# Joining turned sums on GpSimd instead of ScalarE, with more buffers and earlier row loads, in an attention-and-GEGLU block

## The chip, the core and the metric

The kernel runs on one core of a Trainium2 chip. Its engines are TensorE (PE for matmuls and PEld for weight loads in the profile), VectorE (DVE), ScalarE (ACT), GpSimd (POOL) and SyncE (SP), whose queue issues nearly all DMAs. The metric is the time of one execution in device microseconds (us), as the median of several runs.

## What is computed

```python
h = layernorm(x) * (1 + ca) + sa
x = x + ga * attention(h)           # 32 query heads, 8 key/value heads, 512 cached keys, 2048 queries
h = layernorm(x) * (1 + cb) + sb
x = x + gb * ((gelu(h @ w_gate) * (h @ w_up)) @ w_down)
```

`x` is 2048 x 512, the inner width of the second part is 1792, and `sa, ca, ga, sb, cb, gb` are rows of 512 that follow from a condition vector. Everything is float32. The kernel splits each operand into two float16 parts (high and low) and makes three matmuls for one product (`mm3`, L86 to L90).

## The kernel before

The attention part takes some 1330 us of the span and is not touched. The change lies in the second part, the gated network, which the kernel works through in two passes, one for each half of the 2048 rows. A pass is generation g = 0 or 1; it holds 1024 rows, as two blocks `qb` of 512 rows, each of four tiles of 128 rows (QT = 4, QB = 512).

The inner width of 1792 is cut into seven pairs of 128-column tiles (NP = 7). Pair n of a pass has two sets, q = 2n (gate) and 2n + 1 (up). `f_items` (L1264) makes the seven products of a set, in the way of Strassen, in PSUM tiles `fa`, `fb`, `fc`. ScalarE copies them out (L885), VectorE adds and multiplies (L1270, L1287), ScalarE applies the gelu (L1276) and makes the high part of the result `at` (L1297), and the low part is made by L1298, on VectorE or GpSimd.

The product with `w_down` then goes one of two ways:

- The first five pairs of a pass are "turned" (L293). `yt_tasks` (L1696) makes seven products for each of two column halves p, in the order `YORDER`, with the result transposed: the 512 output columns lie along the partitions. `yt_add` (L1653) adds each, scaled by a column, into eight running sums `YT[g, c, qb]` of 128 x 512 (c is the column tile, 0 to 3). They live in the eight buffers of the tag `acc`.
- The last two pairs (NROW = 2) use `y_tasks` (L940): the result lies in rows, in PSUM tiles `py`, and VectorE adds it straight into the tile of rows `acc[ti]` (L952).

After the fifth pair the turned sums must come back to rows. `post` (L1710) sees that a sum got its last addend (`LAST`) and puts off `yt_turn` (L1662). Its `split` (L1666) has ScalarE part the 32-bit sums into low and high 16-bit halves, the "parting" `yu`; its `turn` (L1671) has SP issue a DMA transpose of it into `yv`. There are three buffers for `yu` (tag `qt`). When four sums are parted, the residual rows `y1[ti]` of one block are loaded by `load_acc` (L98) into `acc[ti]`, three ticks later, in buffers of the tag `acc` that parted sums have left. `yt_row` (L1681) then, for each of four row tiles of a block, joins the halves again: ScalarE copies `yv` into `yr` (L1686), a 128 x 1024 copy of 16-bit numbers that takes its two halves from places 1024 bytes apart, and GpSimd adds `yr` to the residual rows (L1687). `yr` lies in the tag `raw`, of five buffers. A tile of rows is written out (L1647 and L1649) when it has this and its two `py` addends (`f_final`, L1641).

What sets the order: the SP queue issues strictly in the order in which the Python code emits. The loop at L1727 emits seven steps for each set and calls `tick` after each; `put_off(n, f)` runs f after n ticks. On the other engines a scheduler places the instructions of this part by its own estimate of times, so the built program's order on them may differ from the order of emission; each engine then works through its own list in order. PSUM has five buffers for the tag `acc` (NACC), which `py`, `fb`, `fc` and the turned products share.

Of the kernel before, what the change touches and what calls it, by code (L numbers as in the profile page):

```python
# [10 lines left out]
F32 = mybir.dt.float32  # L11
F16 = mybir.dt.float16
U16 = mybir.dt.uint16
BF16 = mybir.dt.bfloat16
AF = mybir.ActivationFunctionType
# [3 lines left out]
P = 128  # L19
S, D, F = 2048, 512, 1792  # L20
HQ, HKV, DH = 32, 8, 128
W = 512
KT = D // P
NF = F // P
NT = S // P
QB = 512
QT = QB // P
# [18 lines left out]
NRW = 2  # L46
NWR = 2
# [17 lines left out]
def block_kernel(ctx: ExitStack, tc: tile.TileContext, x, kT, v, wq, wo, wg, wu, wd, cT, wc, wm, out):  # L65
    nc = tc.nc

    const = ctx.enter_context(tc.tile_pool(name="const", bufs=1))
    pool = ctx.enter_context(tc.tile_pool(name="pool", bufs=2))
# [7 lines left out]
    def raw(name):  # L77
        return pool.tile([P, 512], F32, tag="raw", name=name, bufs=NRAW)
# [7 lines left out]
    def mm3(ps, lhi, llo, rhi, rlo, first, last, chain=False, left=False):  # L86

        order = ((lhi, rlo), (lhi, rhi), (llo, rhi)) if left else ((llo, rhi), (lhi, rhi), (lhi, rlo))
        for n, (a, b) in enumerate(order):
            nc.tensor.matmul(ps, a, b, start=first and n == 0, stop=last and n == 2, skip_group_check=chain)  # L90

    acc, moved, bg = {}, [0], []
# [2 lines left out]
        moved[0] += 1  # L95
        nc.sync.dma_start(out_, in_)

    def load_acc(i, src, eng=None):  # L98
        acc[i] = pool.tile([P, D], F32, tag="acc", name="acc", bufs=2 * QT)
        (eng.dma_start if eng else dma)(acc[i], src)  # L100

    def rows_of(t, i):
# [4 lines left out]
    for i in range(QT):  # L107
        load_acc(i, rows_of(x, i), nc.scalar if i < 2 else None)
# [246 lines left out]
    BK, hs, y1 = {}, {}, {}  # L355
# [100 lines left out]
    def put_off(n, fn):  # L456

        waits_.append([n, fn])
# [415 lines left out]
    def banks(st, tags):  # L874
        def bk(k):
            def get():
                if k not in st:
                    st[k] = bank(*tags[k])
                return st[k]
            return get  # L880
        return bk
# [76 lines left out]
    def attn_final(ti):  # L958
        y1[ti] = dram.tile([P, D], F32, name=f"y{ti}")
        dma(y1[ti], acc[ti])  # L960
        if ti < 2 * QT:
            nxt = ti + 2 * QT
            own, steps = ln_tile(2, ti, lambda: acc[ti])
            own()
            for d, fn in zip((1, 5, 8, 9, 10, 12, 13), steps):
                at(("w", now[0] + d), fn)
            at(now[0] + 12, lambda: load_acc(nxt, rows_of(x, nxt)))
        else:
            ln_last(ti - 2 * QT)
# [63 lines left out]
    for i in range(QT, 2 * QT):  # L1033
        load_acc(i, rows_of(x, i))
# [175 lines left out]
    for g in range(NG):  # L1210
# [9 lines left out]
        elif g >= GW and (not half or pr < GW):  # L1220
            sched_set(g, srcs, t0, by, spread)
            if not half:
                a, b, c, d, e, f = SETPOS2 if g == GW else SETPOS
# [312 lines left out]
    with tc.manual_schedule():  # L1536
        begin()
        nexty, invs = [], {}
        for t in range(T + TAIL):
            now[0] = t  # L1540
            u, s = divmod(t, 4)
# [83 lines left out]
    for i in range(2 * QT):  # L1625
        q = 7 * (2 + i // 2) + 3 * (i % 2)
# [7 lines left out]
    for p in range(2):  # L1634
        q = 51 + 14 * p
# [5 lines left out]
    def f_final(ti):  # L1641
        assert ti in back
        halfway[ti] = halfway.get(ti, 0) + 1
        if halfway[ti] <= NROW:
            return
        if ti >= 2 * QT:
            dma(rows_of(out, ti), acc[ti])  # L1647
        else:
            put_off(2, lambda: dma(rows_of(out, ti), acc[ti]))  # L1649

    YT, YR, back, halfway = {}, {}, set(), {}

    def yt_add(n, c, qb, ps):  # L1653
        by = ST["dyc"][:, KT * (n % NP) + c:KT * (n % NP) + c + 1]
        key = (n // NP, c, qb)
        if key in YT:
            nc.vector.scalar_tensor_tensor(YT[key], ps, by, YT[key], op0=ALU.mult, op1=ALU.add)  # L1657
        else:
            YT[key] = pool.tile([P, QB], F32, tag="acc", name="yt", bufs=2 * QT)
            nc.vector.tensor_scalar(YT[key], ps, by, None, op0=ALU.mult)  # L1660

    def yt_turn(g, c, qb):  # L1662

        def split():
            u = YR["u", c, qb] = pool.tile([P, 2, QB], U16, tag="qt", name="yu", bufs=3)
            nc.scalar.activation(u, YT[g, c, qb].bitcast(U16).rearrange("p (r h) -> p h r", h=2), AF.Copy)  # L1666

        def turn():
            if ("t", qb) not in YR:
                YR["t", qb] = pool.tile([P, KT, 2 * QT, P], U16, tag="pt", name="yv", bufs=NPT)  # L1670
            nc.sync.dma_start_transpose(YR["t", qb][:, c], YR.pop(("u", c, qb)).rearrange("p a b -> p (a b)"))  # L1671

        split()
        put_off(3, turn)
        YR["n"] = YR.get("n", 0) + 1
        if YR["n"] % QT == 0:
            for i in range(QT):
                ti = 2 * QT * g + (YR["n"] - 1) % (2 * QT) // QT * QT + i
                put_off(3, lambda ti=ti: load_acc(ti, y1[ti]) or back.add(ti))

    def yt_row(g, qb, i):  # L1681
        t = YR["t", qb].rearrange("p c (h i) q -> p c q h i", h=2)
        ti = 2 * QT * g + QT * qb + i
        assert ti in back
        r = raw("yr")
        nc.scalar.activation(r.bitcast(U16).rearrange("p (c q h) -> p c q h", c=KT, h=2), t[:, :, :, :, i], AF.Copy)  # L1686
        nc.gpsimd.tensor_tensor(acc[ti], acc[ti], r, op=ALU.add)  # L1687
        f_final(ti)
        if i == QT - 1:
            del YR["t", qb]  # L1690

    ADDS = {1: ((0, 0),), 2: ((0, 0),), 6: ((0, 1),), 5: ((1, 1),), 7: ((1, 1),), 4: ((1, 0),), 3: ((0, 1),)}
    YORDER = (1, 2, 6, 5, 7, 3, 4)
    LAST = {2: (0, 0), 7: (1, 1), 3: (0, 1), 4: (1, 0)}

    def yt_tasks(n):  # L1696
        tasks = []
        for p in range(2):
            st = {}
            bk = banks(st, {"a": ("acc", "ya", NACC) if p else ("qa", "ya", 1), "b": ("acc", "yb", NACC), "c": ("acc", "yc", NACC)})  # L1700

            def group(k, p=p, bk=bk):
                a, b = PROD[k]
                x, start = CHAIN[k]
                ci, off = YCOL[a]
                w, t = WO["f", n, ci], A[n, {"b11": "11", "b21": "21", "b22": "22"}.get(b, b)]
                sl = slice(off + p * P, off + (p + 1) * P)
                mm3(bk(x)(), w[:, 0, sl], w[:, 1, sl], t[:, 0, :], t[:, 1, :], start, k in (2, 4, 3), True)

            def post(k, p=p, st=st):  # L1710
                (i, qb), = ADDS[k]
                yt_add(n, 2 * i + p, qb, st[CHAIN[k][0]])
                if n % NP == NP - NROW - 1 and k in LAST:
                    i, qb = LAST[k]
                    c, g = 2 * i + p, n // NP
                    put_off(2 if k in (3, 4) and p == k // 4 else 1, lambda: yt_turn(g, c, qb))
                    if p and k in (3, 4):
                        for r in range(QT):
                            put_off((9 if k == 4 else 13) + r, lambda r=r: yt_row(g, qb, r))

            tasks += [(lambda k=k, f=group: f(k), lambda k=k, f=post: f(k)) for k in YORDER]
        return [tasks[k:k + 2] for k in range(0, len(tasks), 2)]

    YCOL = {"a11": (0, 0), "a12": (0, 256), "s2": (1, 0), "s3": (1, 256), "s4": (2, 0), "s1": (2, 256), "a22": (3, 0)}
# [2 lines left out]
    for q in range(NQ):  # L1727
        n, m = divmod(q, 2)
        its = items(NG + q) if q < 2 else f_items(q)
        for k, pk in enumerate(ORDER):  # L1730
            if (q, pk) not in f_done:
                all_of(its[pk])
            run(("f", q, k))
            tick()
            if n and k == 2 and m == 0 and turned(n - 1):
                nexty += yt_tasks(n - 1)
            if k in ((1, 2, 5, 6) if q < NQ - 1 else (1, 5)):
                y_next()
        if m == 1 and not turned(n):
            for qi, (a, b) in enumerate((("11", "21"), ("12", "22"))):  # L1740
                for i in range(QT):
                    nexty.append(y_tasks((2 * (n // NP) + qi) * QT + i, [lambda n=n, a=a: A[n, a], lambda n=n, b=b: A[n, b]],
                                         [("f", n, 0), ("f", n, 1)], col("dysc", n % NP), f_final))
# [40 lines left out]
```

## Time and profile before

| | |
|---|---|
| median of 3 runs | 1745.58 us (1743.76 to 1745.96) |
| profiled execution | 1743.57 us |
| its span, first to last instruction | 1741.8 us |
| granted TensorE clock | 1.00 throughout |
| second part, pass 0 turned back | about 1485 to 1531 us of the span |
| second part, pass 1 turned back | about 1677 to 1726 us of the span |

Times in the views count from the start of the span. In a row of a timeline the columns are start, duration, engine, line, operation, output and inputs, how many are merged, and in brackets the idle time of the engine before it and what ended that. The table by stretches gives for each stretch its length and the busy time and instruction count of PE, PEld, DVE, ACT and POOL, then the granted clock, the busy share of the DMA engines and GB/s.

### The profile page before, as it was taken

The page shows a single profiled execution, that of the slowest core. Times are in us where ns is not written, and L with a number is a line of the kernel's source. Part 1 is how long each engine was busy: PE and PEld are TensorE (multiplying, and loading weights), DVE is VectorE, ACT ScalarE, POOL GpSimd, SP SyncE. Part 2 cuts the span into 40 slices and gives each one's busy share as a digit, 9 for nine tenths or more (in the row PEclk, how much of TensorE's full clock was granted, in tenths as well). Part 3 has the DMA queues.
Part 4 walks back from the last instruction along what each step waited for, and adds up shares of the span by engine and source line. Part 5 has one row for each costly group of instructions (what it writes and reads, how often), then busy time and mean ns, then how long its engine had stood idle before and what let it go on. Part 6 is the DMA issues. An engine that isn't in the chain of part 4 may idle for free.

```text
span 1741.8 us, 26188 instructions
## 1 busy us (share of the span) xinstructions
PE 1714.7 (98%) x8022; PEld 787.0 (45%) x8022; DVE 1417.6 (81%) x2454; ACT 1258.5 (72%) x2813; POOL 1045.9 (60%) x1266
## 2 busy tenths in 40 slices
PE   7999999999999999999999999999999999999998
PEld 5444444444444444444444444444444444444443
DVE  7898898888888899888888788888886678556674
ACT  6988788888878777898778778787784554643344
POOL 4889778776788884654675665754621558313422
PEclk9999999999999999999999999999999999999999
DMA  7999999999999999999999999899986663743235
GB/s 236 218 205 211 213 214 207 223 206 221 215 217 228 205 205 187 212 213 230 201 219 224 208 223 220 186 235 218 197 180 150 187 177 128 191 139 100 91 97 167
DMA packets 690636, 339.82 MB, mean 195 GB/s; under 512 B 578880, under 2 KB 601408, under 8 KB 690496
## 3 DMA queue, kind: packets, MB, share of 16 engines
q1 hardware_dynamic: 690208, 337.63, 85.5%
q8 instruction: 63, 1.03, 0.3%
q14 instruction: 77, 0.63, 0.1%
q10 hardware_dynamic: 288, 0.52, 0.1%
HBM read 135.66 MB, written 61.87 MB: 113 GB/s over the span
## 4 chain that ended last, share of the span: by engine, by line
PE 82%; ACT 5%; DVE 5%; DMA 3%; POOL 2%; issue 2%; SPq 0%; ACTq 0%; DVEq 0%; POOLq 0%
PE py L90 19%; PE ps L90 17%; PE po L90 17%; PE qa L90 8%; PE fa L90 6%; PE qc L90 4%; PE fc L90 3%; PE ya L90 2%; PE qb L90 2%; PE fb L90 2%; PE yc L90 1%; ACT ee L991 1%; DMA yv<-yu 1%; ACT p L1003 1%; DVE nm L982 1%
## 5 line engine op out<-in xcount | busy, mean ns | idle before, releaser
L991 ACT ACTIVATE ee<-ps,nm 128x512 f32<-128x512 f32 x512 | 350.1, 684 | 191.9 <-DVE nm L982 189.3
L1008 DVE SCALAR_TENSOR_TENSOR p<-ee,rr,p 128x512 f16<-128x512 f32 x512 | 460.0, 898 | 4.5 <-ACT p L1003 3.9
L982 DVE TENSOR_REDUCE nm<-ps 128x1 f32<-128x512 f32 x512 | 350.4, 684 | 106.1 <-PE ps L90 103.2
L90 PE MATMUL ps<-k,qt 128*128 128x512 f16 x1536 | 414.9, 379 | 5.6 <-ACT ee L991 4.4
L1003 ACT ACTIVATE p<-ee,rr 128x512 f16<-128x512 f32 x512 | 364.6, 712 | 19.0 <-DVE rr L999 10.0
L90 PE MATMUL po<-pt,v 128*128 128x512 f16 x1536 | 373.0, 379 | 2.7 <-DVE kmax L183 1.4
L90 PE MATMUL py<-wo,ot 128*128 128x512 f16 x1536 | 371.5, 379 | 0.1
L90 PEld LDWEIGHTS <-w 128*128 128x128 f16 x2184 | 213.3, 98 | 263.3 <-issue 4.7
L90 PEld LDWEIGHTS <-v 128*128 128x128 f16 x1536 | 149.9, 98 | 184.9 <-DMA pt<-p 2.3
L90 PEld LDWEIGHTS <-ot 128*128 128x128 f16 x1536 | 150.3, 98 | 181.7 <-DVE ot L740 0.5
L90 PEld LDWEIGHTS <-qt 128*128 128x128 f16 x1536 | 145.9, 98 | 176.9 <-issue 4.7
L1303 POOL TENSOR_TENSOR fg<-fg 128x512 f32<-128x512 f32 x40 | 51.8, 1295 | 135.6 <-DVE fg L1287 103.0
L740 DVE SCALAR_TENSOR_TENSOR ot<-po,ot 128x512 f16<-128x512 f32 x128 | 87.7, 685 | 39.1 <-ACT ot L739 38.6
L1297 ACT ACTIVATE at<-fg 128x512 f16<-128x512 f32 x86 | 53.4, 625 | 64.8 <-DVE fg L1287 44.5
L991 ACT ACTIVATION_READ_ACCUMULATOR ee<-ps,nm 128x1 f32 x512 | 99.9, 195 | 0.0
L952 DVE SCALAR_TENSOR_TENSOR acc<-py,ysc,acc 128x512 f32<-128x512 f32 x128 | 94.7, 740 | 6.2 <-PE py L90 6.2
L235 POOL TENSOR_TENSOR lw<-lw,half__86 128x1 f32<-128x1 f32 x37 | 23.4, 633 | 104.2 <-DVE lw L185 104.1
L90 PE MATMUL fa<-t,w 128*128 128x512 f16 x336 | 83.6, 379 | 1.9 <-ACT u L885 1.4
L90 PE MATMUL qa<-t,w 128*128 128x512 f16 x348 | 84.9, 379 | 0.0
L397 POOL TENSOR_TENSOR rs<-rs,nhalf 128x1 f32<-128x1 f32 x32 | 18.8, 586 | 103.6 <-DVE rs L391 100.7
L739 ACT ACTIVATE ot<-po 128x512 f16<-128x512 f32 x128 | 73.8, 577 | 5.0 <-PE po L90 5.0
L1657 DVE SCALAR_TENSOR_TENSOR yt<-ya,dyc,yt 128x512 f32<-128x512 f32 x68 | 50.1, 745 | 22.1 <-PE ya L90 21.7
(241 smaller groups left out, 2794.0 us busy)
## 6 DMA issues: line engine op xcount, KB each, us to landing
w<-kept SPq DMA_DIRECT2D x123, 256.0 KB, 3.3
wo<-kept SPq DMA_DIRECT2D x70, 256.0 KB, 3.4
kept<-stage SPq DMA_DIRECT2D x61, 256.0 KB, 3.3
raw<-in_wo SPq DMA_DIRECT2D x56, 256.0 KB, 3.2
kept<-w SPq DMA_DIRECT2D x39, 256.0 KB, 3.4
rw<-in_wq SPq DMA_DIRECT2D x38, 256.0 KB, 3.2
hs<-hf SPq DMA_DIRECT2D x32, 256.0 KB, 2.9
pt<-p SPq DMA_TRANSPOSE x512, 3.5
```

The lines of the kernel that those rows point to most:

```text
L90: nc.tensor.matmul(ps, a, b, start=first and n == 0, stop=last and n == 2, skip_group_check=chain)
L235: nc.gpsimd.tensor_tensor(out, out, half_, op=ALU.pow)
L739: nc.scalar.activation(t[:, 0, :], src, AF.Copy, scale=scale)
L740: return lambda: nc.vector.scalar_tensor_tensor(t[:, 1, :], src, scale, t[:, 0, :], op0=ALU.mult, op1=ALU.subtract)
L952: nc.vector.scalar_tensor_tensor(acc[ti], st["p"], by, acc[ti], op0=ALU.mult, op1=ALU.add)
L982: nc.vector.tensor_reduce(nm, E[t]["ps"], axis=AX.X, op=ALU.max, negate=True)
L991: nc.scalar.activation(e, E[t]["ps"], AF.Exp, bias=E[t]["nm"], scale=1.0, accum_out=sm[:, t % 2:t % 2 + 1])
L1003: nc.scalar.activation(p16[:, 0, :], E[t]["e"], AF.Copy, scale=E[t]["r"])
L1008: nc.vector.scalar_tensor_tensor(p16[:, 1, :], E[t]["e"], E[t]["r"], p16[:, 0, :], op0=ALU.mult, op1=ALU.subtract)
L1297: nc.scalar.activation(t[:, 0, :], g, AF.Copy)
L1303: nc.gpsimd.tensor_tensor(g[o], g[a], g[b], op=ALU.subtract)
L1657: nc.vector.scalar_tensor_tensor(YT[key], ps, by, YT[key], op0=ALU.mult, op1=ALU.add)
```

## The change

Five things change, all in the step that turns the sums back to rows:

- The copy `yr <- yv` in `yt_row` is a `tensor_copy` on GpSimd, where it was an ACTIVATE on ScalarE. The add stays on GpSimd.
- The partings `yu` take turns in two tags, `qt` (three buffers) and `v16` (two buffers, used by the attention part alone).
- The residual rows are loaded at the first and at the fifth of the eight `yt_turn` calls of a pass, at once and not three ticks later. Those of the first block go to buffers of the tags `rw` and `wr` (two each), which the preparation of weights used earlier; those of the second block still go to `acc`.
- For the second column half p = 1, the last two products of `yt_tasks` are swapped: product 4, which completes block 0, comes before product 3, which completes block 1.
- The ticks: `yt_turn` is put off by 2 ticks for product 3 and 1 for the others; `yt_row` by 7 (block 0) and 8 (block 1) ticks, with two rows to a tick, where it was 9 and 13 with one row to a tick.

```diff
-    def load_acc(i, src, eng=None):
-        acc[i] = pool.tile([P, D], F32, tag="acc", name="acc", bufs=2 * QT)
+    def load_acc(i, src, eng=None, tag="acc", bufs=2 * QT):
+        acc[i] = pool.tile([P, D], F32, tag=tag, name="acc", bufs=bufs)
...
         def split():
-            u = YR["u", c, qb] = pool.tile([P, 2, QB], U16, tag="qt", name="yu", bufs=3)
+            tag, bufs = (("qt", 3), ("v16", 2))[YR.get("n", 0) % 2]
+            u = YR["u", c, qb] = pool.tile([P, 2, QB], U16, tag=tag, name="yu", bufs=bufs)
...
+        def rows_in(qb, tags):
+            for i in range(QT):
+                ti = 2 * QT * g + QT * qb + i
+                load_acc(ti, y1[ti], None, *tags[i // 2])
+                back.add(ti)
+
+        done = YR.get("n", 0) % (2 * QT)
+        if done == 0:
+            rows_in(0, (("rw", NRW), ("wr", NWR)))
+        if done == QT:
+            rows_in(1, (("acc", 2 * QT),) * 2)
         split()
         put_off(3, turn)
         YR["n"] = YR.get("n", 0) + 1
-        if YR["n"] % QT == 0:
-            for i in range(QT):
-                ti = 2 * QT * g + (YR["n"] - 1) % (2 * QT) // QT * QT + i
-                put_off(3, lambda ti=ti: load_acc(ti, y1[ti]) or back.add(ti))
...
-        nc.scalar.activation(r.bitcast(U16).rearrange("p (c q h) -> p c q h", c=KT, h=2), t[:, :, :, :, i], AF.Copy)
+        nc.gpsimd.tensor_copy(r.bitcast(U16).rearrange("p (c q h) -> p c q h", c=KT, h=2), t[:, :, :, :, i])
...
-    YORDER = (1, 2, 6, 5, 7, 3, 4)
+    YORDER = ((1, 2, 6, 5, 7, 3, 4), (1, 2, 6, 5, 7, 4, 3))
...
-                    put_off(2 if k in (3, 4) and p == k // 4 else 1, lambda: yt_turn(g, c, qb))
+                    put_off(2 if k == 3 else 1, lambda: yt_turn(g, c, qb))
                     if p and k in (3, 4):
                         for r in range(QT):
-                            put_off((9 if k == 4 else 13) + r, lambda r=r: yt_row(g, qb, r))
+                            put_off((7 if k == 4 else 8) + r // 2, lambda r=r: yt_row(g, qb, r))
```

More of the change, by code (lines that the diff above doesn't have):

```diff
@@ L1715, in post @@
                     c, g = 2 * i + p, n // NP
-                    put_off(2 if k in (3, 4) and p == k // 4 else 1, lambda: yt_turn(g, c, qb))
+                    put_off(2 if k == 3 else 1, lambda: yt_turn(g, c, qb))
                     if p and k in (3, 4):
                         for r in range(QT):
-                            put_off((9 if k == 4 else 13) + r, lambda r=r: yt_row(g, qb, r))
-            tasks += [(lambda k=k, f=group: f(k), lambda k=k, f=post: f(k)) for k in YORDER]
+                            put_off((7 if k == 4 else 8) + r // 2, lambda r=r: yt_row(g, qb, r))
+            tasks += [(lambda k=k, f=group: f(k), lambda k=k, f=post: f(k)) for k in YORDER[p]]
         return [tasks[k:k + 2] for k in range(0, len(tasks), 2)]
```

## The prediction

> **What bounds the kernel now.** I read the page first, for the share of each engine, then the table by stretches over the two places where sums are turned back, then the chain of waits there.
>
> ```profile
> PE 1714.7 (98%) x8022; PEld 787.0 (45%) x8022; DVE 1417.6 (81%) x2454; ACT 1258.5 (72%) x2813; POOL 1045.9 (60%) x1266
> ```
> ```profile
> 1520.00:1525.00 5.00, 4.71 (x23) 2.07 (x22) 2.25 (x4) 5.00 (x7) 4.24 (x4) 1.00 0.71 256
> 1525.00:1530.00 5.00, 4.90 (x23) 1.98 (x22) 2.84 (x5) 4.19 (x7) 2.75 (x3) 1.00 0.00 0
> ...
> 1705.00:1710.00 5.00, 4.77 (x24) 2.06 (x22) 3.44 (x5) 2.13 (x3) 0.00 (x0) 1.00 1.14 303
> 1710.00:1715.00 5.00, 4.14 (x20) 1.76 (x19) 1.44 (x2) 1.79 (x4) 0.00 (x0) 1.00 1.18 244
> ...
> 1720.00:1725.00 5.00, 4.08 (x19) 1.59 (x18) 2.09 (x3) 4.04 (x5) 5.00 (x5) 1.00 0.00 0
> 1725.00:1730.00 5.00, 4.11 (x19) 1.61 (x18) 3.72 (x6) 1.86 (x3) 0.97 (x1) 1.00 0.00 0
> ```
> ```profile
> 1511.80 4.98 DMA yv<-yu
> ...
> 1517.88 4.35 ACT yr L1686 x4
> ...
> 1709.73 4.66 DMA yv<-yu
> ...
> 1715.49 4.35 ACT yr L1686 x4
> ...
> 1720.37 3.19 ACT yr L1686 x3
> ```
>
> TensorE is busy for 98% of the span, so the kernel ends when TensorE has been fed to the end. The chain runs through its matmuls nearly everywhere; it leaves them in the two stretches that the change touches, for transposes and ScalarE's copies. The second number of a row by stretches is TensorE's busy time. It lacks 0.29 + 0.10 us in the first pass, and 0.23 + 0.86 + 0.92 + 0.89 us in the second up to 1730: 3.3 us in all. That is the most that these edits can win there by removing waits, and 0.19% of 1745.58. A matmul's shown time outlasts its step: six take 1.46 us (rows below), one 0.38 (1.46 less five steps of 0.216), so each of some fourteen gaps costs up to 0.16 us more than it shows; counted from start to start the loss is up to 5.6 us.
>
> ```profile
> 1709.73 1.23 SPq L1671 DMA_TRANSPOSE yv<-yu  x1
> ...
> 1713.59 1.47 PE L90 MATMUL fc<-t,w 128*128 128x512 f16 x6 [0.86 <-DMA w<-kept]
> 1714.42 5.43 ACT L1686 ACTIVATE yr<-yv 128x1024 uint16<-128x1024 uint16 x5 [3.21 <-DMA yv<-yu]
> ...
> 1715.67 10.30 POOL L1687 TENSOR_TENSOR acc<-acc,yr 128x512 f32<-128x512 f32 x8 [32.52 <-ACT yr L1686]
> ...
> 1724.09 1.46 PE L90 MATMUL fa<-t,w 128*128 128x512 f16 x6 [0.74 <-ACT u L885]
> ...
> 1726.23 1.46 PE L90 MATMUL fa<-t,x 128*128 128x512 f16 x6 [0.69 <-ACT u L885]
> ...
> 1735.28 3.34 DVE L952 SCALAR_TENSOR_TENSOR acc<-py,dysc,acc 128x512 f32<-128x512 f32 x4 [0.54 <-PE py L90]
> ```
>
> The last transpose is issued at 1709.73 and lands 4.66 us later; ScalarE copies eight tiles, GpSimd adds them until 1725.97. TensorE's waits on `u` come from ScalarE, which had the copies ahead. VectorE's last add ends at 1738.62, and the span at 1741.8: 3.2 us lie behind it.
>
> **The change part by part.** *What ScalarE loses.*
>
> ```profile
> L1686 ACT ACTIVATE yr<-yv x16: 1156/1164/1180, 1516.8 to 1722.4; 128x1024 uint16<-128x1024 uint16 x16
> L1687 POOL TENSOR_TENSOR acc<-acc,yr x16: 1255/1270/1722, 1518.1 to 1724.7; 128x512 f32<-128x512 f32 x16
> ```
>
> Sixteen copies of 1.164 us, 9.3 us a pass, leave ScalarE. In the first pass that gives back the 0.39 us. In the second, one of the two waits on `u` goes (0.9 us of 1.8, since the other is the round trip of a PSUM tile that ScalarE must empty). So 1.3 us.
>
> *The partings and the transposes.* With five buffers ScalarE's waits on `yv<-yu` go (rows of `yu`: 7.8 us in four waits), and the order of the last two products closes block 0 first.
>
> ```profile
> L1666 ACT ACTIVATE yu<-yt x16: 1041/1052/1058, 1485.0 to 1707.9; 128x1024 uint16<-128x1024 uint16 x16
> ...
>   DMA yv<-yu: 7.8, 4
> ```
> ```profile
> 1697.71 0.75 DVE L1657 SCALAR_TENSOR_TENSOR yt<-ya,dyc,yt 128x512 f32<-128x512 f32 x1
> ...
> 1698.20 0.60 ACT L885 ACTIVATE fg<-fa 128x512 f32<-128x512 f32 x1 [1.16 <-PE fa L90]
> ...
> 1699.23 1.46 PE L90 MATMUL py<-wo,at 128*128 128x512 f16 x6
> ...
> 1701.09 1.95 SPq L96 DMA_DIRECT2D acc<-y  x4
> ...
> 1721.09 1.40 DVE L952 SCALAR_TENSOR_TENSOR acc<-py,dysc,acc 128x512 f32<-128x512 f32 x2
> ```
>
> In the built program the third sum of block 0 is the one completed at 1698.46; its parting follows ScalarE's copy from PSUM that ends at 1698.80, so it ends near 1699.9. Behind it SP issues two transposes (1.23 us and a step of 0.05), two weight loads (some 0.47 each, as the four loads of rows take 1.95), a transpose, a load, and then the transpose that closes block 0: 5.3 us, so it goes at 1705.2. With the 4.66 us to landing, GpSimd can start at 1710, 4.4 us before ScalarE does now. The weight load that TensorE awaits at 1713.59 comes earlier too: with the 0.23 near 1707, some 1.1 us won.
>
> *The residual rows.* Eight loads of a pass move forward on SP past weight loads and transposes; the count stays. VectorE's waits on them (`acc<-y`) go. But the second four now stand ahead of a `wo` load that TensorE needs for its `py` at 1699.23: four issues of 0.47 us put it 1.9 us back, less what slack it has. Between nothing and 1.9 I take 1.4 us lost.
>
> *The copies on GpSimd.* No row shows a copy of 1024 numbers there, nor one that reads with a step. The nearest:
>
> ```profile
> L158 POOL TENSOR_SCALAR stage<-rw 128x512 f16<-128x512 f32 x3 | 1.9, 619 | 3.8 <-DMA kept<-stage 3.6
> L158 POOL TENSOR_SCALAR stage<-rw 128x256 f16<-128x256 f32 x1 | 0.4, 406 | 0.1
> ```
> ```profile
> L159 POOL TENSOR_TENSOR stage<-rw,stage 128x512 f16<-128x512 f32 x3 | 3.5, 1156 | 0.3
> L159 POOL TENSOR_TENSOR stage<-rw,stage 128x256 f16<-128x256 f32 x1 | 0.7, 672 | 0.1
> ```
> ```profile
> L239 POOL TENSOR_SCALAR acc<-acc,mv,rs 128x512 f32<-128x512 f32 x7 | 15.8, 2262 | 0.0
> ```
>
> With one input, 256 more elements cost 0.213 us, so 1024 would take 0.619 + 2 x 0.213 = 1.05 us: the lower end. With two inputs 256 cost 0.484 us, so 1024 would take 1.156 + 2 x 0.484 = 2.1 us. The dearest row, 2.26 us for 512, doubled, gives 4.5: the upper end. The copy reads by turns from two places, as the two-input form does, so I take 2.1 us.
>
> [...]
>
> *GpSimd and VectorE get in each other's way.*
>
> ```profile
> 1438.94 1.57 DVE L1287 SCALAR_TENSOR_TENSOR fg<-fg,gsc,u 128x512 f32<-128x512 f32 x1
> 1440.44 0.73 DVE L1287 SCALAR_TENSOR_TENSOR fg<-fg,gsc,fa 128x512 f32<-128x512 f32 x1
> ```
> ```profile
> 1438.81 1.16 POOL L1298 TENSOR_TENSOR at<-fg,at 128x512 f16<-128x512 f32 x1
> 1439.92 1.73 POOL L574 TENSOR_TENSOR cb<-cb 128x512 f32<-128x512 f32 x1
> ```
>
> VectorE's L1287 with two inputs from SBUF started 0.13 us into a GpSimd instruction and took 1.57 us; the same with one input from PSUM took 0.73. GpSimd's next took 1.73 and not 1.27. So a VectorE instruction with two SBUF inputs waits for the running GpSimd instruction, and delays the next by 0.46. In each pass seven such (L1287, L1298) fall into the time of the copies.
>
> *Order.* `yr` has five buffers, so GpSimd does five copies, five adds, three copies, three adds. It adds to a tile after VectorE's first `py` and before a later one, so VectorE stands at L952 for GpSimd, with `at`, `fg` and `u` behind it in its queue and TensorE behind those. For block 1 even the first `py` add now comes after GpSimd's, so four PSUM buffers of five stay full till then, and the last `py` tiles pass through the fifth: a tile's add of 0.75 us and its signals, about 1.0 us, lie bare between its matmuls and the next tile's, for three tiles: 3.0 us.
>
> *The sum, second pass, GpSimd's chain.* Start 1710; eight copies of 2.1 = 16.8; eight adds of 1.27 = 10.2; seven delays of 0.46 = 3.2; end at 1740.2. Then VectorE's last two adds (1.4, as at 1721.09) and the 3.2 behind them: 1744.8, against 1741.8: +3.0. TensorE's own chain: +1.4 + 3.0 for the load and the buffer, -0.9 - 1.1 won: +2.4, a little less. GpSimd's sets the end from a copy of 2.0 us on.
>
> *First pass.*
>
> ```profile
> 1562.91 2.62 POOL L1303 TENSOR_TENSOR fg<-fg 128x512 f32<-128x512 f32 x2 [31.89 <-ACT fg L1276]
> ```
>
> GpSimd's next work comes at 1562.91 and covers its longer turn, but VectorE is not covered. Seven two-input instructions wait for half a copy each, 7 x 1.05 = 7.4 us; VectorE's slack in 1520 to 1530 is 10 - 2.25 - 2.84 = 4.9; 2.5 us come through to TensorE, less the 0.39 won: +2.1, of which I take 1.7, as some of the seven find an add running.
>
> In all +4.7 us: 1743.57 + 4.7 = 1748.3 for a profiled execution. The median of before is 2.0 above its profiled execution, so the median goes to 1745.58 + 4.7 = **1750.3**.
>
> **The rivals.** A measurement can tell about 0.2%, 3.5 us.
>
> *A, the copy is cheap* (1.05 to 1.7 us). For it: one-input rows; ScalarE's copy with the same reads, 1.16 us, is only 0.11 above its other 16-bit copy. GpSimd's chain then ends 3 to 8 us sooner, and TensorE's chain sets the time: +2.4, first pass +0.5 less 0.39: 1748. Within 0.2%.
>
> *B, faster.* The buffers turn over behind other matmuls, the `wo` load has slack, and the freed ScalarE gives back all of TensorE's gaps: from 3.3 to 5.6 us, so 1741. It needs a copy of at most 1.1 us, so that five copies and an add are over by 1717, before the last `at`. Against it: the built order puts `py` adds of block 1 behind others.
>
> [...]
>
> *D, the rows gain nothing*: SP issues in order, so an early load waits for its buffer or is late all the same. Buffers of `rw` and `wr` have been idle since the attention part; the price would be VectorE's old waits on `acc<-y`, already in the time before: about 1750 again.
>
> **How the numbers follow.** Forecast (copy 1.7 to 2.8 us, 1748 to 1758, D within it) 0.48, A 0.34, C 0.13, B 0.05. The range reaches to a copy of 1.05 us with part of the new waits (1745) and to one of 3.2 us (1763); B, the dear end of C and part of A lie outside. Faster takes B, 0.05; same takes A less its slow end and the cheap edge of the forecast, 0.34; slower the rest, 0.61.
>
> **What would show it.** Right: `yr<-yv` on GpSimd near 2.1 us, first at 1710; TensorE's idle gone at 1713, new near 1699 and behind 1725 ahead of `py`, released by VectorE's L952; L1287 and L1298 of VectorE at 1.5 to 2.7 us; GpSimd's last add behind 1737. Wrong: copies near 1.1 us, or over 3, or a GpSimd that is done by 1730 while the span is still longer.

## The result and the profile after

The changed kernel takes 1748.62 us (median of 10 runs, 1746.18 to 1750.74), the kernel before 1743.86 us beside it (10 runs, 1743.23 to 1746.7). The ratio is 1.0025, with a 95% interval of 1.0015 to 1.0035: slower by a quarter of a per cent, 4.4 to 4.8 us. The profiled execution took 1748.56 us with a span of 1746.7 us, 4.9 us more than the span before.

The page's line of busy time, and the table by stretches for the places shown of before:

```profile
PE 1713.2 (98%) x8020; PEld 787.2 (45%) x8022; DVE 1419.5 (81%) x2454; ACT 1241.7 (71%) x2797; POOL 1066.1 (61%) x1282
```
```profile
1520.00:1525.00 5.00, 5.00 (x25) 2.29 (x24) 0.69 (x1) 1.21 (x3) 5.00 (x5) 1.00 0.66 228
1525.00:1530.00 5.00, 5.00 (x25) 2.29 (x24) 1.17 (x2) 1.67 (x3) 5.00 (x5) 1.00 0.03 9
...
1700.00:1705.00 5.00, 2.43 (x12) 1.12 (x12) 1.58 (x3) 1.62 (x2) 0.00 (x0) 1.00 1.14 224
...
1720.00:1725.00 5.00, 4.32 (x21) 1.85 (x20) 0.85 (x2) 0.60 (x1) 5.00 (x5) 1.00 0.00 0
1725.00:1730.00 5.00, 3.34 (x15) 1.35 (x14) 4.96 (x6) 1.26 (x2) 5.00 (x4) 1.00 0.00 0
1730.00:1735.00 5.00, 2.57 (x12) 1.10 (x12) 3.85 (x5) 0.63 (x1) 3.60 (x3) 1.00 0.20 75
```

In the first pass TensorE (second number) is now busy throughout, although GpSimd (fifth busy time) is too. In the second pass it lacks 2.57 us (5.00 - 2.43) in the stretch from 1700 and 4.77 us (0.68 + 1.66 + 2.43) in the three from 1720. The view of TensorE's waits from 1690 on names them. Its columns are who waits for whom, us in total, times, and the longest. First the kernel before, then the changed one:

```profile
PE fa L90 <- ACT u L885: 1.4, 2, 0.7
PE fc L90 <- DMA w<-kept: 0.9, 1, 0.9
PE py L90 <- ACT at L1297: 0.4, 2, 0.2
PE fc L90 <- DVE fg L1270: 0.2, 1, 0.2
```
```profile
PE py L90 <- DMA wo<-kept: 3.2, 1, 3.2
PE py L90 <- DVE acc L952: 2.8, 2, 1.8
PE py L90 <- DVE u L1270: 1.3, 1, 1.3
PE fa L90 <- ACT u L885: 0.7, 1, 0.7
```

2.9 us of waits became 8.0 us: 5.1 more, close to the 4.9 us by which the span grew. The waits on `w` and one of the two on `u` went, as they were meant to. A wait on the `wo` load and waits on VectorE's adds (L952) came. The copy itself, in the view of one line, with minimum, median and maximum in ns:

```profile
L1694 POOL COPY yr<-yv x16: 1135/1152/1621, 1513.2 to 1727.0; 128x1024 uint16<-128x1024 uint16 x16
```

It takes 1.15 us on GpSimd, where ScalarE took 1.16. So two suspects are left: the order of the work, and GpSimd's collisions with VectorE. The timeline around the `wo` load:

```profile
1695.19 1.95 SPq L96 DMA_DIRECT2D acc<-y  x4
...
1697.20 0.42 SPq L96 DMA_DIRECT2D wo<-kept  x1
...
1698.14 6.33 SPq L1672 DMA_TRANSPOSE yv<-yu  x3
...
1702.57 1.46 PE L90 MATMUL py<-wo,at 128*128 128x512 f16 x6 [3.19 <-DMA wo<-kept]
```

The `wo` load goes out 2.1 us later than before (1695.12 there), behind the four row loads, and lands some 5.3 us after its issue. It is also a piece of the profile's chain that ended last (start and duration):

```profile
1697.20 5.33 DMA wo<-kept
```

The timeline of the tail:

```profile
1724.32 4.26 POOL L1694 COPY yr<-yv 128x1024 uint16<-128x1024 uint16 x3
1724.84 1.17 DVE L1287 SCALAR_TENSOR_TENSOR fg<-fg,gsc,u 128x512 f32<-128x512 f32 x1
...
1726.70 0.87 DVE L1298 TENSOR_TENSOR at<-fg,at 128x512 f16<-128x512 f32 x1
...
1728.09 1.04 DVE L1298 TENSOR_TENSOR at<-fg,at 128x512 f16<-128x512 f32 x1
...
1728.55 5.05 POOL L1695 TENSOR_TENSOR acc<-acc,yr 128x512 f32<-128x512 f32 x3
1729.05 1.75 DVE L1287 SCALAR_TENSOR_TENSOR fg<-fg,gsc,u 128x512 f32<-128x512 f32 x1
...
1730.72 0.74 DVE L952 SCALAR_TENSOR_TENSOR acc<-py,dysc,acc 128x512 f32<-128x512 f32 x1
...
1731.52 1.45 PE L90 MATMUL py<-wo,at 128*128 128x512 f16 x6 [1.84 <-DVE acc L952]
...
1733.88 7.93 PE L90 MATMUL py<-wo,at 128*128 128x512 f16 x36 [0.91 <-DVE acc L952]
...
1737.96 5.29 DVE L952 SCALAR_TENSOR_TENSOR acc<-py,dysc,acc 128x512 f32<-128x512 f32 x7 [0.55 <-PE py L90]
```

VectorE's L1287 and L1298, 0.75 and 0.70 us when alone, take up to 1.75 and 1.04 us here, 1.9 us more than alone in the four instructions of this stretch. VectorE makes no `py` add between 1710.0 and 1730.72: in the built program the first `py` adds of block 1 stand behind GpSimd's adds to the same rows. From 1724.12 on VectorE is never idle for GpSimd; it works through these stretched instructions and only then comes to L952. Four of the five PSUM buffers are full in that time, and TensorE waits for the fifth. Then seven adds follow each other without a pause to the end.

### The profile page after: what moved, and what is told of

Its sections match the earlier page's. It is cut to its first block, busy times and chain, and to the rows that moved or that the text cites. A ratio compares the mean times of both kernels' runs of the same rounds, so it can differ in the third digit from the quotient of the medians.

```text
span 1746.7 us, 26159 instructions
## 1 busy us (share of the span) xinstructions
PE 1713.2 (98%) x8020; PEld 787.2 (45%) x8022; DVE 1419.5 (81%) x2454; ACT 1241.7 (71%) x2797; POOL 1066.1 (61%) x1282
## 4 chain that ended last, share of the span: by engine, by line
PE 82%; DVE 5%; ACT 4%; DMA 4%; POOL 3%; issue 1%; SPq 0%; POOLq 0%; DVEq 0%; ACTq 0%
PE py L90 19%; PE po L90 16%; PE ps L90 16%; PE qa L90 8%; PE fa L90 7%; PE qc L90 4%; PE fc L90 3%; PE ya L90 2%; DMA pt<-p 2%; PE qb L90 2%; PE fb L90 2%; ACT ee L991 1%; ACT p L1003 1%; PE yc L90 1%; PE pq L90 1%
## 5 line engine op out<-in xcount | busy, mean ns | idle before, releaser
L952 DVE SCALAR_TENSOR_TENSOR acc<-py,ysc,acc 128x512 f32<-128x512 f32 x128 | 94.7, 740 | 6.2 <-PE py L90 6.2
```

The lines of the kernel that those rows point to most:

```text
L952: nc.vector.scalar_tensor_tensor(acc[ti], st["p"], by, acc[ti], op0=ALU.mult, op1=ALU.add)
```

## The experiments

**Theory 1**: the loss is one of order. The rows of block 1 are joined some ticks earlier in the emission, which puts VectorE's first `py` adds behind GpSimd's adds, and the row loads stand ahead of the `wo` load. **Theory 2**: the engine is the loss, by GpSimd's longer chain and its collisions with VectorE. The median of before is 1744.6 to 1744.8 us beside these runs.

**The copy alone** (the kernel before with one edit):

```diff
-        nc.scalar.activation(r.bitcast(U16).rearrange("p (c q h) -> p c q h", c=KT, h=2), t[:, :, :, :, i], AF.Copy)
+        nc.gpsimd.tensor_copy(r.bitcast(U16).rearrange("p (c q h) -> p c q h", c=KT, h=2), t[:, :, :, :, i])
```

> The kernel before with one edit: the copy yr <- yv on GpSimd in place of ScalarE; buffers, loads, order and ticks as before. Theory 1 (the change loses by order: the residual rows ahead of the wo load, and the sums of block 1 joined ahead of VectorE's first py adds; the engine itself costs little, since the copy takes 1.15 us there and 1.16 on ScalarE): within 1.5 us of before, 1742.5 to 1745.5; VectorE's L1287 and L1298 are stretched by 0.2 to 1 us each beside GpSimd, but TensorE's waits on u go. Theory 2 (GpSimd's longer chain and its collisions with VectorE are the loss): 1747 to 1749, nearly all of the change's +4.8.

Measured: 1743.34 us, ratio 0.9997 (0.9988 to 1.0006). The engine alone costs nothing that can be measured: theory 2 falls in its plain form. The profiled execution was the slowest of the 11 runs (1747.4 us), and its timeline of the first pass says why:

```profile
1528.57 8.77 DVE L1287 SCALAR_TENSOR_TENSOR fg<-fg,gsc,u 128x512 f32<-128x512 f32 x1
```
```profile
1523.68 6.17 POOL L1687 TENSOR_TENSOR acc<-acc,yr 128x512 f32<-128x512 f32 x5
1529.79 3.33 POOL L1686 COPY yr<-yv 128x1024 uint16<-128x1024 uint16 x3
1533.08 3.71 POOL L1687 TENSOR_TENSOR acc<-acc,yr 128x512 f32<-128x512 f32 x3
```

One VectorE instruction of 0.75 us took 8.77 us: it stood until GpSimd's whole row of instructions was done at 1536.8. The last section comes back to it. What the other runs of this kernel met is not seen, since only this one was profiled.

**The copy back on ScalarE** (the changed kernel, the edit above the other way round):

> The changed kernel with one edit: the copy yr <- yv back on ScalarE; five buffers, early rows, swap and ticks stay. Theory 1: the wait of TensorE for the wo load near 1700 stays at about 3.3 us shown; VectorE's first py adds of block 1 still come behind GpSimd's adds, but these end some 8 x 1.15 us sooner, so that the tail gives back most of its 2.7 us: 1744 to 1747. Theory 2: everything comes back: 1743 to 1744.

Measured: 1744.67 us, ratio 0.9998 (0.9989 to 1.0007). All of the loss is gone, though the order of emission stays and the wait on `wo` is still there (1.9 us). VectorE's first `py` adds of block 1, still behind GpSimd's adds, now come in time:

```profile
1715.38 9.09 POOL L1695 TENSOR_TENSOR acc<-acc,yr 128x512 f32<-128x512 f32 x7 [0.27 <-ACT yr L1694]
```
```profile
1720.82 0.75 DVE L952 SCALAR_TENSOR_TENSOR acc<-py,dysc,acc 128x512 f32<-128x512 f32 x1 [1.17 <-POOL acc L1695]
...
1722.08 0.75 DVE L952 SCALAR_TENSOR_TENSOR acc<-py,dysc,acc 128x512 f32<-128x512 f32 x1
...
1724.95 1.40 DVE L952 SCALAR_TENSOR_TENSOR acc<-py,dysc,acc 128x512 f32<-128x512 f32 x2
```

The number lies in theory 1's range, 1744 to 1747, but that everything comes back is what theory 2 said; with the first run it says that neither the engine nor the order is enough.

**The late join** (the changed kernel with the old ticks of block 1):

```diff
-  put_off((7 if k == 4 else 8) + r // 2, lambda r=r: yt_row(g, qb, r))
+  put_off(7 + r // 2 if k == 4 else 13 + r, lambda r=r: yt_row(g, qb, r))
```

> The changed kernel with one edit: the rows of block 1 joined 13 + r ticks after the product, as before, and not 8 + r // 2, so that the built order has VectorE's first py add of block 1 ahead of GpSimd's; GpSimd keeps its copies. Theory 1: TensorE's waits on VectorE's L952 near 1731 and 1734 go (1.84 + 0.91 us shown) and the row of adds behind the last matmul shrinks; the wo wait stays: 1744 to 1746. Theory 2: GpSimd has the same 16 copies and adds, so no more than 1 us comes back: 1747.5 to 1749.

Measured: 1744.44 us, ratio 1.0 (0.9991 to 1.0009). The loss is gone again, with all sixteen copies on GpSimd. GpSimd's last add ends at 1732.8, hardly earlier than in the changed kernel (1733.6), but VectorE's first adds of block 1 stand at 1718.38, 1721.92, 1723.22 and 1724.51, ahead of it. No wait on L952 is left:

```profile
PE py L90 <- DMA wo<-kept: 2.5, 1, 2.5
PE py L90 <- ACT at L1297: 1.0, 2, 0.9
```

**The rows behind the `wo` load** (the changed kernel):

```diff
-            rows_in(1, (("acc", 2 * QT),) * 2)
+            put_off(3, lambda: rows_in(1, (("acc", 2 * QT),) * 2))
```

> The changed kernel with one edit: the four residual rows of block 1 loaded three ticks later, behind the wo and w loads on SP. Theory 1: the wait for the wo load near 1700 (3.19 us shown) goes or falls below 1 us; if the tail is then set by TensorE, 1745.5 to 1747; if GpSimd and VectorE set the tail whatever TensorE does before, the gain is lost again there and it stays at 1748 to 1749. Theory 2: 1748 to 1749.

Measured: 1750.51 us, ratio 1.0037 (1.0024 to 1.005), above what either theory expected. The wait on `wo` is gone, and nothing is won; it came back in the tail:

```profile
PE py L90 <- DVE acc L952: 4.2, 2, 3.3
PE py L90 <- DVE u L1270: 1.0, 1, 1.0
PE fa L90 <- DMA w<-kept: 0.9, 1, 0.9
```

TensorE came to the tail 1.4 us earlier (its last group of `fa` starts at 1722.71, in the changed kernel at 1724.14) and waited longer for L952: 4.2 us, where the changed kernel waits 2.8. The timeline shows two reasons:

```profile
1729.66 0.86 DVE L1298 TENSOR_TENSOR at<-fg,at 128x512 f16<-128x512 f32 x1 [0.70 <-ACT at L1297]
...
1730.45 0.74 DVE L952 SCALAR_TENSOR_TENSOR acc<-py,dysc,acc 128x512 f32<-128x512 f32 x1
...
1731.24 2.72 PE L90 MATMUL py<-wo,at 128*128 128x512 f16 x6 [3.28 <-DVE acc L952]
```

In this build VectorE's list has an L1298, with its wait for ScalarE, ahead of L952: 0.70 us of waiting and 0.86 of work that stand behind L952 in the changed kernel. And the six matmuls behind the long pause took 2.72 us, where the changed kernel's took 1.45 (granted clock 0.50 from 1731 to 1733). So the edit moved VectorE's order along with the loads, and what the 3.2 us wait for `wo` is worth in the changed kernel is not shown.

**Both edits, copies on GpSimd**:

> The changed kernel with both edits of the runs before it: rows of block 1 joined at 13 + r, and their residual rows loaded three ticks later, behind the wo load; the copies stay on GpSimd. Theory 1 (order): in the run with the ticks alone TensorE lost 4.4 us between 1690 and 1723, nearly all at the wo load and in the half-rate matmuls behind it; with the load in front this falls to the 1 to 2 us of waits on w that the run with the rows alone shows there, and the tail keeps its 1.3 us: 1741 to 1743, the fastest so far, 0.1 to 0.2% under before. Rival (GpSimd's chain sets the end at about 1733 in any case, so that what TensorE gains earlier is lost in the tail again, as in the run with the rows alone): 1744 to 1745.

Measured: 1744.3 us, ratio 1.0 (0.9989 to 1.0011), and a wide spread, 1740.71 to 1751.32 in 12 runs. Theory 1 foretold 1741 to 1743: missed. Its rival's 1744 to 1745 held.

**Both edits, copies on ScalarE**:

> The same with the copies back on ScalarE. Theory 1: the engine does not matter once the join is late: within 1 us of the run with the copies on GpSimd, 1741 to 1744. Rival (the engine is the gain or the loss): 2 us or more apart.

Measured: 1741.64 us, ratio 0.9984 (0.9975 to 0.9992): faster than the kernel before. The distance to the run with the copies on GpSimd is 2.7 us. Theory 1 expected less than 1 us and its rival 2 us or more, so here too the rival held; but the two intervals still touch. TensorE's waits in this run:

```profile
PE fa L90 <- DMA w<-kept: 1.5, 1, 1.5
PE py L90 <- ACT at L1297: 0.2, 1, 0.2
```

**The early join alone, on each engine** (the kernel before; with GpSimd's copy in the first of the two):

```diff
-  put_off((9 if k == 4 else 13) + r, lambda r=r: yt_row(g, qb, r))
+  put_off(9 + r if k == 4 else 8 + r // 2, lambda r=r: yt_row(g, qb, r))
```

> The kernel before with two edits: the copy on GpSimd, and the rows of block 1 joined at 8 + r // 2 ticks in place of 13 + r; loads, buffers and the order of products as before. Theory 1: the early join puts VectorE's first py adds of block 1 behind GpSimd's adds, four of the five PSUM buffers stay full, and the loss of the change is there without its other parts: 1747 to 1750, 3 to 5 us above the kernel with the copy on GpSimd alone. Rival (the loss needs the early rows or the swap): within 1.5 us of before.

> The kernel before with one edit: the rows of block 1 joined at 8 + r // 2 ticks; the copy stays on ScalarE. Theory 1: the same wait of VectorE on GpSimd's adds, but these end some 9 us sooner, since eight copies of 1.15 us are elsewhere; the wait then ends while TensorE still has other work: 1743.5 to 1746. Rival (the early join alone costs it): 1747 to 1750.

Measured: with GpSimd's copy 1754.52 us, ratio 1.0054 (1.0042 to 1.0066); with ScalarE's 1746.1 us, ratio 1.0008 (0.9999 to 1.0016). The second is just above theory 1's range (1743.5 to 1746) and below its rival's. The first is beyond what was expected:

```profile
1731.89 11.96 PE L90 MATMUL py<-wo,at 128*128 128x512 f16 x42 [3.61 <-DVE acc L952]
...
1743.89 2.73 DVE L952 SCALAR_TENSOR_TENSOR acc<-py,dysc,acc 128x512 f32<-128x512 f32 x4 [0.54 <-PE py L90]
```

In this kernel block 1 is completed first, and the last three adds of block 0 come behind all others. And the 42 matmuls behind the wait on L952 took 2.7 us more than 42 do at the usual step of 0.216 us; the granted clock was 0.50 from 1732 to 1736 (0.996 over this whole execution, 1.00 in the kernel before). The four ratios to the kernel before make a table:

| kernel before with | copy on ScalarE | copy on GpSimd |
|---|---|---|
| late join (13 + r) | 1 | 0.9997 |
| early join (8 + r // 2) | 1.0008 | 1.0054 |

Neither edit alone can be told from no change; both together cost 0.5%. They make a loss of the same kind without the early rows, the five buffers or the swap. It is twice that of the change, in part by the half-rate matmuls.

**What the place of the row loads and the join are worth on ScalarE**. Both kernels are the changed one with ScalarE's copy; the first has the old ticks, the second the rows behind the `wo` load:

> The changed kernel with the copies back on ScalarE and the rows of block 1 joined at 13 + r; its residual rows stay ahead of the wo load. It differs from the fastest run so far (1741.6) in that load alone. Theory 1: with a tail that neither GpSimd nor VectorE sets, TensorE's wait for the wo load near 1700 (1.9 to 3.2 us in the runs that have the rows in front, against 1.5 us of waits on w in the one that has not) shows in the time: 1743 to 1745, 1 to 3 us slower than the fastest. Rival (the tail takes up what is lost at 1700): 1741 to 1742.5.

> The changed kernel with the copies back on ScalarE and the residual rows of block 1 behind the wo load; the early join stays. It differs from the fastest run so far in the ticks of block 1 alone. Theory 1: on ScalarE the early join costs little (0.8 of a thousand in the kernel before): 1742 to 1744. Rival (the early join costs on either engine once the load is not in its way): 1745 to 1748.

Measured: 1743.97 us, ratio 0.9995 (0.9986 to 1.0004), with the row loads in front of `wo`; 1742.05 us, ratio 0.9986 (0.9978 to 0.9995), with the early join. Both lie where theory 1 expected them. So on ScalarE the place of the row loads makes 2.3 us (1743.97 against 1741.64; the intervals overlap a little), and the early join 0.4 us (1742.05 against 1741.64), which is within the noise.

But the profiles do not show the 2.3 us at the `wo` load. From 1690 on TensorE waits 1.8 us with the rows in front (1.2 of it for `wo`), and 1.7 us in the fastest run (1.5 of it for `w`). What differs is a wait in the first pass, here with the rows in front:

```profile
1514.14 6.49 ACT L1694 ACTIVATE yr<-yv 128x1024 uint16<-128x1024 uint16 x6 [3.82 <-DMA yv<-yu]
...
1520.54 0.57 ACT L885 ACTIVATE fg<-fa 128x512 f32<-128x512 f32 x1
...
1521.16 1.46 PE L90 MATMUL fa<-t,x 128*128 128x512 f16 x6 [2.04 <-ACT fg L885]
```

Six copies in a row stand ahead of ScalarE's copy out of PSUM, for which TensorE waits 2.04 us; in the fastest run four do, and it does not wait there. So this edit, too, moved the order on another engine. The mechanism that theory 1 gave for the 2.3 us, the wait for `wo`, is not borne out by these two profiles.

## Why the prediction was right, and where its working was not

The time was: 4.7 us more were forecast, and the medians lie 4.8 apart. The working was not. Point by point:

- **The copies on GpSimd**, 2.1 us each: the step that failed. They took 1.15 us, near the lower end from the one-input rows (1.05), and as rival A held. The reason given, that the copy reads by turns from two places as a two-input form does, is refuted by that row. The upper ends of the forecast and of the range, 1758 and 1763, stand on copies of 2.8 and 3.2 us, which no run shows: the sixteen of the changed kernel took 1.14 to 1.62 us.
- **GpSimd's chain sets the end**: wrong. It was to end at 1740.2 and ended at 1733.6, and the late join took the loss away while that chain ended at 1732.8. In the changed kernel TensorE's `py` and VectorE's adds set the end.
- **First pass**, +1.7: nothing was lost. TensorE is busy for all of 1520 to 1530, with copies of 1.15 us.
- **The residual rows**, 1.4 us lost at the `wo` load: the wait came there but was 3.2 us, because the load also landed late. What it is worth in the changed kernel is open: the run that undid it there won nothing, but in it VectorE's order and a half-rate stretch changed as well. On ScalarE the rows behind `wo` gave 2.3 us, which the profiles show at another wait.
- **Order**, 3.0 us for `py` tiles that pass through the one free PSUM buffer: the right mechanism. The rows show 2.8 us of waits on L952 and 1.3 us on `u` behind stretched VectorE instructions. What the prediction didn't see is the edit that causes it: it is the ticks, 8 in place of 13, together with GpSimd's copies. Each was undone alone, and each gave back the whole loss. The five buffers and the swap were not undone alone.
- **What is won**: one of the two waits on `u` (0.7 us as shown) and the 0.9 us wait on `w` did go, as said.
- **Rival A** (cheap copy, TensorE's chain sets the time) is what happened, with +4.8 where it was given +2.5. That the forecast hit its number is luck: a copy nearly twice too dear made up for waits of TensorE that were priced too low, 2.4 us where the views show 5.1. Its 1750.3 us also stood on a median of before of 1745.58, from three runs; beside the changed kernel it was 1743.86.

Theory 1 as it was put after the result, that the engine costs little, holds for the late join (0.9997) and not for the early one. How much GpSimd's copies cost in the best order is left open, between nothing and 2.7 us.

## What to carry to other kernels

Where two engines add to the same tile, see which add the order of emission puts first. Here the join that is emitted earlier made VectorE's adds, and the PSUM buffers that they would empty, wait for GpSimd's chain: TensorE waited 2.8 us on L952 in the changed kernel, and not at all with the late join. Before pricing a move to another engine, ask which instruction now stands behind it; here neither the move nor the earlier join cost anything that can be told alone (0.9997 and 1.0008), and both together cost 0.5% (1.0054). And do not book a wait in the profile at its length: the edit that removed 3.2 us of waiting also moved VectorE's list and won nothing. After each edit of the emission order, look again at the order that the scheduler built on every engine.

## What the runs showed of the hardware

VectorE's L1287 with two inputs from SBUF outlasted the GpSimd instruction beside which it started: in the tail above one took 1.75 us in place of 0.75, and ended 0.55 us after the add that ran at its start (1728.55, 1.70 us). In the run with the copy alone one stood for 8.77 us, until the running add and seven more instructions were done, and ended 0.55 us after the last (rows above). It starts at 1528.57, some 0.01 us ahead of the fifth of the five adds (their row ends at 1529.85, and an add takes 1.27 us). The longest L1287 in the profiles of the kernel before and of the changed one took 1.57 and 1.75 us. It may be the long case that spreads the times of the kernels with GpSimd's copies (1740.71 to 1751.32 in one); that was not shown.

TensorE's granted clock fell to 0.50 around some pauses, and not around every one. In the run with the late join, TensorE idled for 2.53 us before 1703.20, and the table by stretches shows (last but two, the granted clock):

```profile
1702.00:1704.00 2.00, 0.80 (x4) 0.37 (x4) 0.00 (x0) 0.91 (x1) 0.00 (x0) 0.94 1.18 251
1704.00:1706.00 2.00, 2.00 (x6) 0.68 (x5) 1.31 (x2) 0.17 (x1) 0.00 (x0) 0.50 1.22 244
1706.00:1708.00 2.00, 2.00 (x8) 0.84 (x7) 0.19 (x1) 1.21 (x2) 0.00 (x0) 0.70 0.97 228
```
```profile
1703.20 2.20 PE L90 MATMUL py<-wo,at 128*128 128x512 f16 x6 [2.53 <-DMA wo<-kept]
1705.19 2.45 PE L90 MATMUL fa<-t,w 128*128 128x512 f16 x6
```

Groups of six that take 1.46 us took 2.20 and 2.45: 1.7 us on top of the wait. In the changed kernel the pause of 3.19 us at the same place left the clock at 1.00. So one pause of 2.53 us came with a halved clock and one of 3.19 us without; what decides it no run here shows.
